# Pooled attention and a SiLU MLP in one kernel: queries transposed as pairs of 4 bytes, scores over even and odd dimensions, and two changes of order in the last tiles

## Chip, cores and metric

The kernel runs on one core of a Trainium2 chip. The metric is device time in microseconds. Before the change it is 284.45 us, the median of three runs (284.24 to 284.8). The profiled execution took 284.22 us; its profile covers a span of 282.3 us, and the TensorE clock was granted in full (1.0) throughout. All positions below are microseconds from the start of that span.

## What is computed

The reference works on 8 batches of 8 heads, 576 positions and a head dimension of 64, and then on 4608 tokens of width 512:

```python
k_p = k.reshape(B, H, Sp, 8, D).mean(axis=3)          # 576 keys pooled to 72
v_p = v.reshape(B, H, Sp, 8, D).mean(axis=3)
attn = softmax(q @ k_p.T / sqrt(D))
x = (attn @ v_p).transpose(0, 2, 1, 3).reshape(4608, 512)
h = x @ w_in                                          # 512 -> 2048
out = (h * sigmoid(h)) @ w_out                        # 2048 -> 512, float32
```

## The kernel before

**Tiles.** The MLP runs in nine tiles of 512 tokens, `t` = 0 to 8 (loop at L804). Each tile has an up phase (`up`, L470: `x @ w_in`, SiLU into `h_T`) and a down phase (`down` for tile 0, `down_quarters`, L642, for the others). The attention of batch `a = t + 1` is spread through the phases of tile `t`; batch 0 comes ahead of the loop, in a preamble (L746 to L780) in which `warm_up` matmuls fill the waits on TensorE.

**Order.** Every engine runs its instructions in the order in which the program emits them. `spread` (L416) counts the steps of a phase (a step is one or two matmuls), and a filler given as `(step, function)` is emitted right after the matmul of that step. So a number such as 71 or 103 in the loop places an instruction in the queue of its engine.

**Products with seven multiplications.** The down phase of tiles 1 to 8, and parts of the up phase, form a product of two 2x2 block matrices from seven block products instead of eight. They need sums of blocks: `hidden_sum` (L612, from `h_T` into `h_sum`), `unit_x_sum` (L452, from `xT` into `x_sum`), `weight_sum` and `unit_weight_sum`. All of them run on VectorE (DVE). In the up phase such a product is a unit, and its stages are named 2, 5, 1, 4, 3, 7, 6 for the block products, and `h` and `s` for the two SiLUs that read `c_sb`. The results of 7 and 6 pass DVE (L519, L522: `c_sb` = PSUM + `t_sb`), and `t_sb` comes from L507 and L510, so that each unit has a chain of four dependent DVE operations. `c_sb`, `t_sb` and `rr_sb` are shared by the units.

**Tiles 7 and 8** use three units, A, B and C, and four plain groups `g0` to `g3` of four 512-column matmuls (`plain`, L537). Their order is written out by hand in the strings `THREE` (L799): the first string is that of tile 7 (`t = B - 1`), the second that of tile 8. In both, the groups that a unit's SiLUs write lie in other parts of `h_T`: A and B in the upper half of each half of the hidden dimension, which the first two block products of the down phase read (L665, L666), and C and the plain groups in the lower.

**Down phase.** `down_quarters` begins with block products 2 and 5, each in two parts (upper half, then lower half), and goes on with 1, 4, 3, 7 and 6. Each needs its `h_sum`. In the last tile the block products after 5 are done for output rows 0 to 127 of each half first (`cc = (0,)`) and then for the others, so that the stores at the end are small. There, product 6 for the first rows takes steps 64 to 71, and `hidden_sum(6, 0, 4)` (L843) is placed after step 71: these matmuls are emitted ahead of the sum of that half.

**Queries.** `q_transpose` (L155) takes a tile `q_bf` whose partitions hold (head, 32 positions) and whose columns hold (i, d), and transposes 32x32 blocks of bf16 on DVE, 576 columns at a time. Four such operations serve a batch. The result `qT` is laid out `[.., i, c, p]`, where `c` is the half of the head dimension, 0 to 31 or 32 to 63, and each 32-row group of partitions is one head.

**Scores.** `scores` (L342) multiplies, for each head, the pooled keys `kz` (32 rows) with `qT` (32 rows): two matmuls, one for each `c`, add up in PSUM. Four heads lie in four row groups of the array. The keys come as `kz[.., c, :]` from `k_transpose` (L216, batches 3 to 7, out of the pooled `kp`) or `select_k` (L288, batches 0 to 2, out of `k5`).

Of the kernel before, what the change touches and what calls it, by code (L numbers as in the profile page):

```python
# [27 lines left out]
FP32 = mybir.dt.float32  # L28
FP32R = mybir.dt.float32r
BF16 = mybir.dt.bfloat16  # L30
# [6 lines left out]
def kernel(  # L37
# [11 lines left out]
    B, H, S, D = q.shape  # L49
    POOL = 8  # L50
    SP = S // POOL
# [14 lines left out]
    QP = 32  # L66
    QI = S // QP
    QF = QI // 2
    DH = D // 2
# [12 lines left out]
    singles = ctx.enter_context(tc.tile_pool(name="singles", bufs=1))  # L82
    big = ctx.enter_context(tc.tile_pool(name="big", bufs=1))
    mid = ctx.enter_context(tc.tile_pool(name="mid", bufs=2))
# [37 lines left out]


    kz = [singles.tile([128, 2, 2, SP], BF16, name=f"kz{n}") for n in range(2)]
    kp = singles.tile([128, 2, 2, 4, DH], BF16, name="kp")

    batches = {}

# [5 lines left out]
    def load_q(b, halves=False):  # L134
        st = batches.setdefault(b, {})
        q_bf = mid.tile([128, 2, QI * D], BF16, tag="q_bf", name="q_bf")
        if halves:
            pass
        elif b == B - 1:

            for s in range(4):
                for a in range(2):
                    nc.gpsimd.dma_start(
                        out=q_bf[QP * s : QP * (s + 1), a, :].rearrange(
                            "p (i d) -> p i d", d=D
                        ),
                        in_=q[b, 4 * a + s].rearrange("(i p) d -> p i d", p=QP),
                    )
        else:
            nc.gpsimd.dma_start(out=q_bf, in_=q_r[b])  # L150
        st["q_bf"] = q_bf
        st["qT"] = mid.tile([128, 2, QI, 2, QP], BF16, tag="qT", bufs=1, name="qT")


    def q_transpose(b, a, f):  # L155
        st = batches[b]
        n = QF * D
        nc.vector.transpose(  # L158
            out=st["qT"][:, a, f * QF : (f + 1) * QF].rearrange("r i c p -> r (i c p)"),
            in_=st["q_bf"][:, a, f * n : (f + 1) * n],  # L160
        )


# [28 lines left out]
    def add_rest(dst, raw):  # L192
        nc.vector.tensor_add(
            out=dst,
            in0=raw[:, :, :D].rearrange("k h (c d) -> k h c d", c=2),
            in1=raw[:, :, D : 2 * D].rearrange("k h (c d) -> k h c d", c=2),
        )

    def pool_k(b, stage):
        st = batches[b]  # L200
        raw = st["k_raw"]
        if stage == 0:
            add_halves(raw)
            return
        for i in range(2):
            add_rest(
                kp[:SP, i].rearrange("k c s d -> k s c d"), raw[:, 4 * i : 4 * (i + 1)]
            )

    def pool_v(b):  # L210
        st = batches[b]
        st["vp"] = mid.tile([SP, H, D], BF16, tag="vp", name="vp")
        add_halves(st["v_raw"])
        add_rest(st["vp"].rearrange("k h (c d) -> k h c d", c=2), st["v_raw"])

    def k_transpose(b, parts=(0, 1)):  # L216
        st = batches[b]
        kT_ps = ps_tile([128, 2, 2, SP], FP32, "at", "kT_ps")
        for a in parts:
            for c in range(2):  # L220
                nc.tensor.matmul(
                    kT_ps[:, a, c, :],
                    lhsT=kp[:, a, c].rearrange("k s d -> k (s d)"),
                    rhs=ident[:, :SP], start=True, stop=True,
                )
        a0, a1 = parts[0], parts[-1] + 1
        nc.scalar.copy(kz[b % 2][:, a0:a1], kT_ps[:, a0:a1])
# [7 lines left out]
    k5, v5 = (singles.tile([128, SLOTS + 1, D], BF16, name=f"{n}5") for n in "kv")  # L235
# [52 lines left out]
    def select_k(b, a):  # L288
        st = batches[b]
        if a == 0:  # L290
            st["kz_ps"] = ps_tile([128, 2, 2, SP], FP32, "at", "kz_ps")
        for c in range(2):
            for s in range(4):
                for i, r, sp, m in segments(4 * a + s):
                    nc.tensor.matmul(
                        st["kz_ps"][32 * s : 32 * (s + 1), a, c, sp : sp + m],
                        lhsT=k5[:, i, c * DH : (c + 1) * DH],
                        rhs=ident[:, r : r + m], start=True, stop=True,
                    )

# [31 lines left out]
    def width(segs):  # L332
        return QP * sum(i1 - i0 for _, i0, i1 in segs)
# [8 lines left out]
    def scores(b, segs):  # L342
        st = batches[b]
        w = width(segs)
        sc = [ps_tile([128, 512], FP32, "at", "sc_ps")[:SP, :w] for s in range(4)]
        for g, i0, i1, cs in seg_cols(segs):
            for c in range(2):
                for s in range(4):
                    rows = slice(32 * s, 32 * (s + 1))
                    nc.tensor.matmul(  # L350
                        sc[s][:, cs],
                        lhsT=kz[b % 2][rows, g, c, :],
                        rhs=st["qT"][rows, g, i0:i1, c, :],
                        start=(c == 0), stop=(c == 1),
                    )
        es = mid.tile([SP, 4, VW], BF16, tag="es", bufs=4, name="es")[:, :, :w]
        for s in range(4):
            nc.scalar.activation(es[:, s, :], sc[s], func=AF.Exp, scale=score_scale)  # L358
        st["es", segs] = es
# [92 lines left out]
    def unit_x_sum(t, n):  # L452
        a, b = U_X[n]
        nc.vector.tensor_tensor(
            out=x_sum[:, U_XI[n]], in0=x_quarter(t, *a), in1=x_quarter(t, *b),
            op=ALU.subtract if n in (3, 4) else ALU.add,
        )
# [154 lines left out]
    def hidden_sum(n, k0, k1):  # L612
        a, b, op = H_SUMS[n]
        ks = slice(k0, k1)
        nc.vector.tensor_tensor(  # L615
            out=h_sum[n][:, ks, :], in0=quarter(*a, ks), in1=quarter(*b, ks), op=op
        )
# [175 lines left out]
    def load_half_2(name, half):  # L793
# [1 line left out]
            load_slots(nc.gpsimd, 2, name, i0, i1, half)  # L795

    THREE = (
        "g0 A2 A5 g1 A4 B2 A3 A1 B5 A7 C2 A6 B4 B3 B1 C5 Ah B7 As C4 Bh B6 C1 C3 C7 Bs"
        " g2 C6 Ch Cs g3",  # L799
        "A2 A5 g0 A4 B2 A3 A1 B5 A7 C2 A6 B4 B3 B1 C5 Ah B7 As C4 Bh B6 C1 C3 C7 Bs g1"  # L800
        " C6 Ch Cs g2 g3",
    )
# [1 line left out]
    for t in range(NT):  # L804
        a = t + 1
        f_up, f_down = [], []
        if t == 0:
            GA = 11
            items = [(g, 0, HS) for g in range(GA)]
            items += [(g, HS, NTT - HS) for g in range(GA)]  # L810
            items += [(g, 0, NTT) for g in range(GA, KG)]
            f_up += [(1, lambda: denominators(0, part(0, 1), on_dve=True))]
            f_up += [(5, lambda: denominators(0, part(1, 1), on_dve=True))]
            f_up += [(13, lambda: numerators(0, part(0, 1)))]
            f_up += [(17, lambda: numerators(0, part(1, 1)))]
        else:
            G = lambda *gs: [(g, 0, NTT) for g in gs]
            if t == 1:
                items = (
                    G(12, 13, 14, 15) + [(0, "251")] + G(8) + [(0, "43")] + G(9)  # L820
                    + [(0, "7h6")] + G(10) + [(0, "s")] + G(11, 0, 1, 2, 3)
                )
            elif t >= B - 1:
                items = []
                for it in THREE[t - B + 1].split():
                    items += [(("BCA".index(it[0])), it[1])] if it[0] in "ABC" else G(int(it[1]))
            else:
                items = (
                    G(12, 13) + [(0, "251")] + G(14) + [(0, "43")] + G(15) + [(0, "76")]
                    + [(1, "2")] + [(0, "hs")] + [(1, "51")] + G(0) + [(1, "43")] + G(1)  # L830
                    + [(1, "7h6")] + G(2) + [(1, "s")] + G(3)
                )
            if t < B - 1:
                for n in U_X:
                    f_up.append((0, lambda n=n: unit_x_sum(t, n)))
            for n in (2, 5):
                h_at = {B - 1: 54, B: 50}.get(t, 36 if t > 1 else 45)
                f_up.append((h_at, lambda n=n: hidden_sum(n, 4, 8)))
            f_up.append((56, lambda: hidden_sum(6, 4, 8)))
            for n, k0 in ((2, 0), (5, 0), (1, 4), (1, 0)):  # L840
                f_up.append((64, lambda n=n, k0=k0: hidden_sum(n, k0, k0 + 4)))
            f_down.append((33, lambda: hidden_sum(7, 0, 8)))
            f_down.append((71, lambda: hidden_sum(6, 0, 4)))  # L843

        for n, t0, f_to, at, parts in (
            (1, 0, f_down, 48, (0, PW)), (3, 0, f_down, 52, (0, PW)),
# [61 lines left out]
                    f_down.append((nu_at[n], lambda: numerators(a - 1, visits[2])))  # L908
        if t in (B - 2, B - 1):
            for n in (4, 1, 3, 7, 6):  # L910
                f_down.append((103 if t < B - 1 else 44, lambda n=n: unit_x_sum(t + 1, n)))
        if t == B - 2:
            k_w = big.tile([128, 4, 2, 256], BF16, tag="k_raw2", name="w_sum12")
            v_w = big.tile([128, 4, 2, 256], BF16, tag="v_raw2", name="w_sum12")
# [37 lines left out]
```

The softmax here doesn't subtract the row's maximum and nothing guards it: scores larger than these inputs give would overflow.

## Time and profile before

| what | value | from |
|---|---|---|
| median time | 284.45 us | three runs |
| span of the profile | 282.3 us | page |
| preamble, up to the first matmul of tile 0 | 16.8 us | timeline of TensorE |
| tile 7, up phase to first matmul of down phase | 228.3 to 241.7 us | timeline of TensorE |
| tile 8, the same | 254.0 to 266.6 us | timeline of TensorE |
| last matmul begins, with its row of 8 | 278.2 us | timeline of TensorE |
| stores and end | 279.3 to 282.3 us | stretches of time |

The profile is a page of one execution and views of its trace. A group of instructions is told by line, engine, operation and tile, with its busy time and the mean duration of one. The chain of waits is followed back from the last instruction: at each step to what released it, or to the instruction before it on its engine. [...]what one costs in a stream is the distance between starts. A row of eight 256-column matmuls, for example, starts 0.87 us before the next row.

### The profile page before, as it was taken

What the parts mean: (1) busy time and instruction counts of PE and PEld (TensorE: products, weight loads), DVE (VectorE), ACT (ScalarE), POOL (GpSimd) and SP (SyncE); (2) the same over time, 40 slices, a digit from 0 to 9 for tenths busy, and PEclk for the clock granted to TensorE, in tenths of its full rate; (3) what the DMA queues carried; (4) which work ended last, traced back from release to release, by engine and by line L of the source; (5) the groups of instructions that cost most, each with busy time, mean ns of one, the idle gap of its engine ahead of it and who ended that gap; (6) DMA issues with size and microseconds to landing.
All of it is one profiled execution on the core that took longest, in us unless ns stands there. A gap on an engine that the chain in (4) does not pass through costs nothing.

```text
span 282.3 us, 6969 instructions
## 1 busy us (share of the span) xinstructions
PE 274.7 (97%) x2803; PEld 197.5 (70%) x2823; DVE 232.3 (82%) x418; ACT 184.5 (65%) x361; POOL 61.2 (22%) x79
## 2 busy tenths in 40 slices
PE   7899999999999999999999999999999999999995
PEld 4348544556777677767888786688667778688784
DVE  4987946899978898879887988799888978966973
ACT  1678765667577866787668856885779477326800
POOL 8745217332140214021402130441100000000001
PEclk9999999999999999999999999999999999999999
DMA  7999999896659843986397539597830041005004
GB/s 208 286 266 230 214 316 167 222 192 110 138 79 214 158 116 46 187 186 127 67 186 187 96 85 178 136 142 108 135 101 0 2 103 48 2 2 128 23 2 149
DMA packets 31312, 37.70 MB, mean 134 GB/s; under 512 B 10352, under 2 KB 22256, under 8 KB 31280
## 3 DMA queue, kind: packets, MB, share of 16 engines
q0 software_dynamic: 23920, 27.03, 53.7%
q1 hardware_dynamic: 6928, 9.58, 12.1%
q10 hardware_dynamic: 432, 0.66, 0.6%
q8 instruction: 22, 0.36, 0.5%
q14 instruction: 10, 0.08, 0.1%
HBM read 36.70 MB, written 9.44 MB: 163 GB/s over the span
## 4 chain that ended last, share of the span: by engine, by line
PE 90%; DVE 5%; DMA 2%; issue 1%; ACT 1%; DVEq 0%
PE hp_ps L547 23%; PE o_psP L655 16%; PE o_psQ L655 15%; PE u_psP L487 7%; PE u_psQ L487 7%; PE o_psR L655 5%; PE sc_ps L350 4%; PE o_ps L582 3%; PE nu_ps L394 3%; PE u_psR L487 2%; PE den_ps L368 2%; DMA raw<-in_k_dram 2%; DVE xT L403 1%; PE warm_ps L704 1%; DVE w_sum L633 1%
## 5 line engine op out<-in xcount | busy, mean ns | idle before, releaser
L547 PE MATMUL hp_ps<-xT,w_in_sb 128*128 128x512 bf16 (+3 forms) x365 | 72.3, 335 | 0.9 <-issue 0.2
L655 PEld LDWEIGHTS <-h_sum 128*128 128x128 bf16 x640 | 60.5, 98 | 12.8 <-DVE h_sum L615 1.9
L553 ACT ACTIVATE h_T<-hp_ps 128x512 bf16<-128x512 f32 (+2 forms) x87 | 46.5, 541 | 19.0 <-PE hp_ps L547 16.9
L615 DVE TENSOR_TENSOR h_sum<-h_T 128x1024 bf16<-128x1024 bf16 (+1 forms) x72 | 50.6, 745 | 5.0 <-ACT h_T L553 5.0
L547 PEld LDWEIGHTS <-w_in_sb 128*128 128x128 bf16 x380 | 36.2, 98 | 21.6 <-issue 0.6
L358 ACT ACTIVATE es<-sc_ps 72x384 bf16<-72x384 f32 (+1 forms) x100 | 39.0, 469 | 9.9 <-PE sc_ps L350 9.8
L487 PEld LDWEIGHTS <-w_sum 128*128 128x128 bf16 x340 | 33.3, 98 | 7.5
L655 PEld LDWEIGHTS <-h_T 128*128 128x128 bf16 x256 | 24.1, 98 | 4.4 <-issue 0.9
L403 DVE TENSOR_TENSOR xT<-nu_ps,rec 128x384 bf16<-128x384 f32 (+1 forms) x50 | 23.9, 532 | 0.2
L495 ACT ACTIVATE h_T<-c_sb 128x512 bf16<-128x512 f32 x34 | 20.6, 626 | 5.2 <-DVE c_sb L519 5.0
L377 ACT ACTIVATE lnd<-den_ps 128x384 f32<-128x384 f32 (+1 forms) x23 | 11.1, 483 | 19.4 <-PE den_ps L368 19.4
L158 DVE STREAM_TRANSPOSE qT<-q_bf 128x576 bf16<-128x576 bf16 x32 | 23.0, 755 | 0.6 <-DMA q_bf<-in_q_dram 0.6
L182 POOL DMA_DIRECT2D raw<-in_k_dram x5 | 7.1, 1429 | 52.1 <-DMA raw<-in_k_dram 52.1
L273 DVE TENSOR_TENSOR raw<-raw 128x384 f32<-128x384 f32 (+3 forms) x20 | 12.3, 618 | 7.2 <-DMA raw<-in_v_dram 4.1
L655 PE MATMUL o_psP<-w_out_sb,h_sum 128*128 128x256 bf16 x128 | 17.7, 273 | 0.6 <-DVE h_sum L615 0.6
L559 POOL DMA_DIRECT2D out_dram<-o_sb x2 | 1.2, 591 | 78.1 <-issue 77.3
L655 PE MATMUL o_psQ<-w_sum,h_sum 128*128 128x256 bf16 x128 | 16.7, 273 | 0.0
L504 ACT COPY r_sb<-u_psP 128x512 f32<-128x512 f32 x17 | 9.9, 584 | 10.2 <-PE u_psP L487 7.6
L655 PE MATMUL o_psQ<-w_out_sb,h_sum 128*128 128x256 bf16 x128 | 16.6, 273 | 0.0
L510 DVE TENSOR_TENSOR t_sb<-u_psR,rr_sb 128x512 f32<-128x512 f32 x17 | 11.8, 692 | 5.8 <-PE u_psR L487 4.1
L655 PE MATMUL o_psQ<-w_sum,h_T 128*128 128x256 bf16 x128 | 16.5, 273 | 0.0
L655 PE MATMUL o_psP<-w_sum,h_T 128*128 128x256 bf16 x128 | 16.5, 273 | 0.0
(83 smaller groups left out, 464.7 us busy)
## 6 DMA issues: line engine op xcount, KB each, us to landing
out_dram<-o_sb SPq DMA_DIRECT2D x128, 64.0 KB, 3.9
raw<-in_k_dram POOLq DMA_DIRECT2D x10, 576.0 KB, 9.6
raw<-in_v_dram POOLq DMA_DIRECT2D x10, 576.0 KB, 8.0
q_bf<-in_q_dram POOLq DMA_DIRECT2D x6, 576.0 KB, 12.7
w_in_sb<-in_moe_w_in_dram POOLq DMA_DIRECT2D x8, 256.0 KB, 8.6
w_out_sb<-in_moe_w_out_dram POOLq DMA_DIRECT2D x4, 512.0 KB, 13.4
raw<-in_v_dram POOLq DMA_DIRECT2D x2, 768.0 KB, 11.1
raw<-in_k_dram POOLq DMA_DIRECT2D x1, 768.0 KB, 10.3
```

The lines of the kernel that those rows point to most:

```text
L158: nc.vector.transpose(out=st["qT"][:, a, f * QF : (f + 1) * QF].rearrange("r i c p -> r (i c p)"), in_=st["q_bf"][:, a, f * n : (f + 1) * n],)
L273: nc.vector.tensor_add(out=raw[..., :w], in0=raw[..., :w], in1=raw[..., w : 2 * w])
L350: nc.tensor.matmul(sc[s][:, cs], lhsT=kz[b % 2][rows, g, c, :], rhs=st["qT"][rows, g, i0:i1, c, :], start=(c == 0), stop=(c == 1),)
L358: nc.scalar.activation(es[:, s, :], sc[s], func=AF.Exp, scale=score_scale)
L403: nc.vector.tensor_mul(out=xT[:, 2 * g0 + c : 2 * (g0 + ng - 1) + c + 1 : 2, cols], in0=nu[c][:, :w].rearrange("r (g n) -> r g n", g=ng), ...
L487: nc.tensor.matmul(ps[y, bank][:, u, :], lhsT=w[:, kk, 128 * u : 128 * (u + 1)], rhs=x[:, kk, :], start=first and u == 0 and kk == 0, stop ...
L495: nc.scalar.activation(h_T[:, g : g + 2, j * NQ : (j + 1) * NQ], src, func=AF.Silu)
L510: tt(out=t_sb, in0=ps[y, "R"], in1=rr_sb, op=ALU.subtract)
L547: nc.tensor.matmul(hp_ps[:, r0:r1], lhsT=w_in_sb[:, kk, g * 128 : (g + 1) * 128], rhs=xT[:, kk, x0 : x0 + r1 - r0], start=(kk == 0), stop= ...
L553: nc.scalar.activation(h_T[:, g, n0 : n0 + n], hp_ps[:, :n], func=AF.Silu)
L615: nc.vector.tensor_tensor(out=h_sum[n][:, ks, :], in0=quarter(*a, ks), in1=quarter(*b, ks), op=op)
L655: nc.tensor.matmul(ps[b][:, c, :], lhsT=left(n, kt, c), rhs=W_OUT[n][:, kt, :], start=b not in begun, stop=kt == k1 - 1, skip_group_check= ...
```

## The change

The queries are transposed as units of 4 bytes, that is, pairs of neighbouring bf16 values: half as many elements pass DVE. Each 32x32 block then covers 32 positions and all 64 dimensions of a head, so that `qT` is laid out `[.., i, p, 2]` and a row holds dimensions 2r and 2r + 1. The two matmuls of a score then run over the even and the odd dimensions, and read `qT` at every second element. The keys follow: `k_transpose` and `select_k` take every second column as stationary operand. `kp` has the plain layout (head, dimension), so that one DVE operation writes it instead of two.

Tile 7 gets another order of its three units, with two plain groups after `C6`, and `g0` after `A5`. The sums of x for tile 7 come at step 98 of tile 6 instead of 103, ahead of the last third of the attention. In tile 8 the sum of the lower half for product 6 comes at step 50, ahead of the matmuls that read it.

```diff
-    kp = singles.tile([128, 2, 2, 4, DH], BF16, name="kp")
+    kp = singles.tile([128, H, D], BF16, name="kp")
...
-        st["qT"] = mid.tile([128, 2, QI, 2, QP], BF16, tag="qT", bufs=1, name="qT")
+        st["qT"] = mid.tile([128, 2, QI, QP, 2], BF16, tag="qT", bufs=1, name="qT")
...
         nc.vector.transpose(
-            out=st["qT"][:, a, f * QF : (f + 1) * QF].rearrange("r i c p -> r (i c p)"),
-            in_=st["q_bf"][:, a, f * n : (f + 1) * n],
+            out=st["qT"][:, a, f * QF : (f + 1) * QF]
+            .rearrange("r i p c -> r (i p c)").bitcast(FP32),
+            in_=st["q_bf"][:, a, f * n : (f + 1) * n].bitcast(FP32),
         )
...
-        for i in range(2):
-            add_rest(
-                kp[:SP, i].rearrange("k c s d -> k s c d"), raw[:, 4 * i : 4 * (i + 1)]
-            )
+        add_rest(kp[:SP], raw)
...
-                    lhsT=kp[:, a, c].rearrange("k s d -> k (s d)"),
+                    lhsT=kp[:, 4 * a : 4 * (a + 1)].rearrange("k s d -> k (s d)")[:, c::2],
...
-                        lhsT=k5[:, i, c * DH : (c + 1) * DH],
+                        lhsT=k5[:, i, c::2],
...
-                        rhs=st["qT"][rows, g, i0:i1, c, :],
+                        rhs=st["qT"][rows, g, i0:i1, :, c],
...
     THREE = (
-        "g0 A2 A5 g1 A4 B2 A3 A1 B5 A7 C2 A6 B4 B3 B1 C5 Ah B7 As C4 Bh B6 C1 C3 C7 Bs"
-        " g2 C6 Ch Cs g3",
+        "A2 A5 g0 B2 A4 A1 A3 B5 C2 A7 B4 A6 Ah B1 B3 As C5 B7 C4 B6 Bh C1 C3 C7 Bs g1"
+        " C6 Ch Cs g2 g3",
         "A2 A5 g0 A4 B2 A3 A1 B5 A7 C2 A6 B4 B3 B1 C5 Ah B7 As C4 Bh B6 C1 C3 C7 Bs g1"
         " C6 Ch Cs g2 g3",
     )
...
-            f_down.append((71, lambda: hidden_sum(6, 0, 4)))
+            f_down.append((71 if t < B else 50, lambda: hidden_sum(6, 0, 4)))
...
-                f_down.append((103 if t < B - 1 else 44, lambda n=n: unit_x_sum(t + 1, n)))
+                f_down.append((98 if t < B - 1 else 44, lambda n=n: unit_x_sum(t + 1, n)))
```

## The prediction

> **What bounds the kernel now.** I read the busy times first, then the waits of TensorE, then the chain of waits around the few waits that are left.
>
> ```profile
> span 282.3 us, 6969 instructions
> ...
> PE 274.7 (97%) x2803; PEld 197.5 (70%) x2823; DVE 232.3 (82%) x418; ACT 184.5 (65%) x361; POOL 61.2 (22%) x79
> ```
>
> TensorE (PE) is busy 97% of the span. A busy PE may still be stretched, so I compared starts: rows of eight 256-column matmuls are 0.87 us apart in tile 2 as in tile 8 (0.109 each), a 512-column one takes 0.216, and that holds from 20.8 us on. Here are PE's waits from 20.8 to 240 us, the whole list (total, times, longest):
>
> ```profile
> PE o_ps L582 <- issue: 0.2, 1, 0.2
> PE hp_ps L547 <- issue: 0.2, 1, 0.2
> ```
>
> In 219 us PE waits for no engine. Work removed from DVE there buys nothing. What can be won lies ahead of 20.8 us and behind 240. The same view from 228 to 283 us has one wait of PE and the weight loads' waits beside it:
>
> ```profile
> PEld L655 <- DVE h_sum L615: 1.6, 4, 1.1
> ...
> PE o_psP L655 <- DVE h_sum L615: 0.6, 1, 0.6
> ```
>
> The chain of waits shows where it lies (start, us, what):
>
> ```profile
> 240.31 0.69 DVE c_sb L522
> 241.00 0.61 DVE h_sum L615
> 241.61 0.05 issue
> 241.66 1.05 PE o_psP L655 x8
> ...
> 265.07 1.73 PE hp_ps L547 x8
> 266.80 0.87 PE o_psP L655 x8
> ```
>
> At the end of tile 7's up phase the chain leaves PE for DVE and comes back at 241.66. At the same place in tile 8 it stays on PE: two plain groups (x8, 1.73 us) run while DVE makes the sum.
>
> In the preamble the chain runs through one of the changed transposes:
>
> ```profile
> 14.82 0.41 DVE vp L320
> 15.23 0.70 DVE qT L158
> 15.93 0.04 issue
> 15.97 0.44 PE sc_ps L350 x8
> 16.41 0.54 PE warm_ps L704 x2
> 16.95 0.25 PE hp_ps L547 x2
> ```
>
> **What the Trainium skill says.** "Vector Engine (DVE) Microarchitecture Reference", "The reshape front-end and per-opcode configuration": a transpose passes one element per cycle and lane, so what counts is elements, not bytes. The group below agrees for 2-byte elements; no row shows 4-byte ones. "SBUF — State Buffer", in "Door 1: The DMA port swizzle", notes lines of 16 bytes and says that one can stride for free inside them, 8 bf16 elements; here the stride is 2. No matmul of this trace reads its moving operand with a stride. "TensorE: Matmul & The Clock Gate", "Weight-path perf modes": the fast load of 128-column weights reads them "packed or strided". The trace agrees for 32 columns: L394 loads `vp` at every second column in 96 ns, L368 the contiguous `ones` in 93.
>
> **The change part by part.**
>
> Transposes:
>
> ```profile
> L158 DVE STREAM_TRANSPOSE qT<-q_bf 128x576 bf16<-128x576 bf16 x32 | 23.0, 755 | 0.6 <-DMA q_bf<-in_q_dram 0.6
> ```
>
> DVE adds in float32 take 692 ns for 512 columns (L507) and 425 for 256 (L690): 1.04 ns a column and 0.16 us fixed. 576 x 1.04 + 160 = 760, against 755, so a transpose passes one element at the same rate. With 288 elements I take 288 x 1.04 + 160 = 460 ns; if 4 bytes took two turns it stays at 755. Saved: 32 x 0.295 = 9.4 us of DVE. `kp`: five times 2 x 414 ns become one of 687 (the same form as `vp`, L193), 0.7 us. Nearly all of these 10 us are worth nothing, since PE waits for no DVE from 20.8 to 240 us.
>
> The preamble has four transposes on DVE's queue, at 7.18, 9.22, 11.73 and 15.15. The time that the first three give back is swallowed here:
>
> ```profile
> 12.69 1.15 DVE L273 TENSOR_TENSOR raw<-raw 128x512 f32<-128x512 f32 x2 [0.19 <-DMA raw<-in_v_dram]
> ```
>
> DVE already waits at 12.69 for a transfer that no edit moves (issued 4.84, 7.8 to landing); it will only wait longer. Ahead of that, PE is tied to its own warm-up matmuls and to ACT's chain. The fourth transpose, from 15.15, counts in full: it ends 0.295 earlier, PE is through with the eight `nu_ps` (from 15.29, 0.36 for such a row) at 15.65, so the scores go from 15.97 to about 15.66, the two warm-ups follow, and the first real matmul goes from 16.79 to 16.48. It needs the two L403 products too: after the transpose they start at about 15.66, when `nu_ps` is ready, at a pitch of 0.35, and end at 16.45. I take **0.29 us**. It is kept afterwards: the silus of tile 0 start behind the same scores, and the weights have landed (the third chunk of `w_in` at 20.7, needed at 22.5; the last of `w_out` at 42.6, needed at 43.4).
>
> Scores: the same 368 matmuls. A row of 16 with 192 columns takes 0.46 us; its columns, four row groups side by side, are 16 x 192 / 4 = 768 at 2.37 per ns (512 in 0.216) = 0.32. If the strided read is free, nothing changes; if it halves the rate, 0.32 a row. I take **0**, from the SBUF page. Weight loads with stride: 20 of 128 columns (98 ns) and 72 of 32 columns; upper bound the float32 load of the preamble (L708, 191 ns): 20 x 0.093 = 1.9 us. I take 0.
>
> Tile 7. In the old order, four plain matmuls run from 240.04 to 240.90, then PE stands until 241.66: 0.76 us. The next four rows of eight take 3.61 us (241.66 to 245.27), in tile 8 3.50 (266.64 to 270.14): 0.11 more, waiting for later sums. In the new order `C6` is followed by two groups, 8 x 0.216 = 1.73. From `C6`'s start to the first sum in use takes 241.66 - 239.60 = 2.06; PE has 0.44 + 1.73 = 2.17 to do. So the gap closes, with 0.11 to spare: **0.87 us** won. Does the order stall earlier? I laid the queues out by hand from the start of the phase (s = 228.28, stages of 0.437, groups 0.86): `B2`'s copy on ACT waits for `rr_sb` of A (231.2), so `A4`'s SiLU ends at 232.28, and `A7`, which needs it, is due at s + 4.36 = 232.64. `A1` needs the bank that L690 frees at 230.5, due 230.89. DVE's chain: `t_sb` of C at 237.5, its `c_sb` at 238.4, and the last `c_sb` is bound by `C6` (239.18 + 0.27 = 239.45), not by DVE. Least room 0.3 us; nothing stalls.
>
> Sums of x at step 98: they swap places with two L403 products (2 x 0.5 us); L690 behind both stays at 229.8. The delayed products free banks for `B5` (231.8) and `C2` (232.2), and would be done at 229.9. Cost 0.
>
> Tile 8's sum (0.60 pitch) now stands ahead of the copy L682: 272.80 to 273.48, so the copy ends at 273.82 instead of 273.39. Behind that copy stands product 6, which writes the same bank and was due at 273.81; 0.05 after the copy is 273.87: **0.06 us** lost, all on the path, as nothing waits between there and the stores.
>
> Sum: 0.87 + 0.29 - 0.06 = 1.10; 284.45 - 1.10 = **283.35 us**.
>
> **Rivals.**
>
> Strided reads slow the scores. For it: no row shows such a read, and PE is the bound, so every ns counts. Against: the SBUF page. At half rate: 21 rows of 192 columns x 0.32 = 6.7, and of the four 288-column rows only the last one on the path, 0.24: 283.35 + 6.9 = 290.3, slower. With a small price, 0.04 us a row, 284.2: no difference.
>
> The new order of tile 7 brings a stall of its own (a bank or ACT late by 0.3 to 0.5), while the end closes. For it: ACT is 0.7 busy there and the room 0.3. Time 283.65 to 283.9.
>
> The preamble gives nothing, because 4-byte transposes take as long, or the first matmul waits for L403: 283.6 to 283.65.
>
> **Chances.** Forecast 0.66; preamble without gain 0.08; a stall in tile 7 0.07 (a third of it within 0.2%); small price of the strides 0.07; full price 0.12. Leaving out the full price and part of the small one, the range goes to 284.2 above; below, to 282.8, for the spread of three runs (0.5 us) and a little more in the preamble. The bound of 0.2% is 0.57 us, 283.88. Faster 0.79, same 0.09, slower 0.12.
>
> **What would show it.** Transposes of 288 elements at 0.46 us; DVE busy 222; PE from the last plain matmul of tile 7 to the next without a gap, `h_sum` gone from PE's waits; first `hp_ps` at 16.5; `sc_ps` rows still 0.46 us. Rows of 0.6 us or more, or PE waiting on `h_T` or `c_sb` in tile 7's up phase, would make it wrong.

## The result, and the profile after

| | before | after |
|---|---|---|
| median time, us | 284.51 (6 runs, 284.24 to 285.54) | 283.34 (6 runs, 283.06 to 283.57) |
| span of the profile, us | 282.3 | 281.3 |
| first matmul of tile 0 | 16.79 | 16.94 |
| first matmul of tile 7's down phase | 241.66 | 240.72 |
| last row of eight begins | 278.18 | 277.20 |

The ratio is 0.9953, with a 95% interval of 0.9938 to 0.9969: 1.34 us less (0.88 to 1.76); the medians themselves are 1.17 apart. The forecast was 283.35, 1.10 us less. The total is right. Some of its parts are not: two that it had at nothing are not nothing, one was not in it, and they partly cancel.

The busy times of the page after:

```profile
span 281.3 us, 6986 instructions
...
PE 276.4 (98%) x2823; PEld 198.1 (70%) x2823; DVE 223.2 (79%) x413; ACT 184.7 (66%) x361; POOL 61.6 (22%) x79
```

DVE has 9.1 us less to do (232.3 before; the forecast had 222) and the span is 1.0 shorter. The group of the transposes, from the list of groups (busy us, mean ns):

```profile
L158 DVE STREAM_TRANSPOSE qT<-q_bf 128x288 f32<-128x288 f32 x32 | 13.4, 453 | 0.3 <-DMA q_bf<-in_q_dram 0.3
```

Half the elements take 453 ns, where the forecast had 460. From 16 us to the end the list of TensorE's waits holds a single entry (who waits for whom: total, times, longest), and its row starts in the preamble, at 15.73; in the list of all engines from 228 on, the weight loads wait for `h_sum` for 0.4 us, where it was 1.6:

```profile
PE nu_ps L391 <- DVE vp L317: 0.2, 1, 0.2
```

The chain of waits after (start, us, what), at the end of tile 7:

```profile
238.72 0.44 PE u_psQ L484 x4
239.16 1.73 PE hp_ps L544 x8
240.89 0.87 PE o_psP L652 x8
```

Tile 7 now stays on TensorE: `C6`, two plain groups, first product, as in tile 8. In tile 8's down phase, products 3, 7 and 6 of the first rows (timeline of TensorE):

```profile
270.85 1.04 PE L652 MATMUL o_psQ<-w_sum,h_T 128*128 128x256 bf16 x8
271.90 1.03 PE L652 MATMUL o_psP<-w_sum,h_sum 128*128 128x256 bf16 x8
272.83 1.03 PE L652 MATMUL o_psQ<-w_sum,h_sum 128*128 128x256 bf16 x8
```

The duration of a row, 1.04, reaches past the start of the next one, so it is the starts that count. Product 7 starts 1.05 behind product 3 and product 6 0.93 behind product 7, where an undisturbed row takes 0.87: product 7 still waits for 0.17, as before, and product 6 for 0.06, which is new. The preamble:

```profile
15.26 0.42 DVE vp L317
15.68 0.04 issue
15.73 0.43 PE nu_ps L391 x8
16.16 0.41 PE sc_ps L347 x8
```

The transpose that stood between `vp` and the scores has left the chain; `nu_ps`, which ran beside it, has taken its place. From the start of the `vp` copy to the first matmul of tile 0 it is 1.68 us (15.26 to 16.94), and 1.97 before (14.82 to 16.79). That stretch is 0.29 shorter, but it begins 0.44 later, because of a transfer: the two DVE adds that wait for it (L270 after, L273 before) come at 13.13, after a wait of 0.68, and before at 12.69, after one of 0.19. Over the profiles of this study without a doubled transpose in the preamble, the `vp` copy begins between 14.82 and 15.68 with bf16 transposes (mean of four 15.23) and between 14.83 and 15.26 with pairs (mean of seven 15.08). I read the 0.44 as the spread of the landing and not as a price of the change.

A gain that the forecast did not have lies in the down phase of tile 1. The timelines of TensorE and DVE, first before:

```profile
69.62 0.78 DVE L158 STREAM_TRANSPOSE qT<-q_bf 128x576 bf16<-128x576 bf16 x1
...
70.09 0.72 PE L350 MATMUL sc_ps<-qT,kz 32*72 32x192 bf16 x16
...
70.74 1.16 PE L655 MATMUL o_psR<-w_sum,h_sum 128*128 128x256 bf16 x9
```

and after:

```profile
69.75 0.47 DVE L158 STREAM_TRANSPOSE qT<-q_bf 128x288 f32<-128x288 f32 x1
...
70.21 0.54 PE L347 MATMUL sc_ps<-qT,kz 32*72 32x192 bf16 x16
70.67 1.16 PE L652 MATMUL o_psR<-w_sum,h_sum 128*128 128x256 bf16 x9
```

Before, the score row takes 0.65 to the start of the next row, after 0.47, as in the other tiles: its second half had waited for the transpose that ends at 70.40. Four microseconds later the same delay reaches `nu_ps` through the `vp` copy on DVE: the copy begins at 73.54 before and at 73.36 after, and the row of `nu_ps` takes 0.60 to the next start (74.10 to 74.70) before and 0.50 after (74.03 to 74.53). Together 0.29. This is the fourth transpose of tile 1, placed at step 2 of the down phase, behind the sums of tile 1 and of the weights. A row ahead of it gains 0.08 too: the first part of product 5 takes 1.05 to the next start before (66.91 to 67.96) and 0.97 after (67.11 to 68.08), because the product behind it waits for its `h_sum`. In the kernel before, DVE goes straight from the first three transposes of tile 1 (58.22 to 60.31) through `c_sb` to that sum; in the kernel after it is idle for 0.71 behind the three.

Two rows of `den_ps`, in tiles 4 and 6, get shorter as well: 0.36 and 0.37 to the next start before, 0.28 after. First tile 4's row before, then the `c_sb` of DVE ahead of it, before and after:

```profile
157.56 0.42 PE L368 MATMUL den_ps<-es,ones 72*32 72x384 bf16 x4
...
151.84 0.69 DVE L519 TENSOR_TENSOR c_sb<-u_psP,t_sb 128x512 f32<-128x512 f32 x1 [0.97 <-ACT h_T L553]
...
151.39 0.69 DVE L516 TENSOR_TENSOR c_sb<-u_psP,t_sb 128x512 f32<-128x512 f32 x1 [0.63 <-ACT h_T L492]
```

The row needs the last `es` of ACT, which ends at 157.61 before, and ACT is late because `c_sb` is: it starts 0.84 after the SiLU that ACT begins at 151.00, and after the change 0.49 after the same SiLU (150.90). These 0.35 are not work that was saved. Counted over all records of DVE in the trace, its semaphore instructions with them and from 0, the late `c_sb` of tiles 4 and 6 are numbers 319 and 447. Number 191 (`t_sb` in tile 2, at 91.09) has the same pause: it starts 0.40 after its semaphore instruction has ended, and 0.04 is usual. The three lie 128 apart. In the kernel after, these numbers fall on other operations, and none of them is held up. So the 0.17 us of the two rows come from the place where the pause falls; what makes it, the traces don't show.

One thing gets longer. A score row of tile 2, before and after:

```profile
99.57 0.53 PE L350 MATMUL sc_ps<-qT,kz 32*72 32x192 bf16 x16
...
99.42 0.54 PE L347 MATMUL sc_ps<-qT,kz 32*72 32x192 bf16 x16
```

The next row starts at 100.03 and at 99.89. Over all undisturbed rows of 16 from tile 1 on, the distance to the next start is 0.458 us before (17 rows) and 0.469 after (18 rows), and no row is more than 0.003 off. The other kernels below agree: 0.458 in each that reads `qT` without a stride, 0.469 in each that reads every second element. That is 0.0105 us a row, 0.22 us for the 21 rows of 192 columns. The strided reads are not quite free.

### The profile page after: what moved, and what is told of

The parts are those of the page before. It is cut to its first block, busy times and chain, and to the rows that moved or that the text cites. A ratio compares the mean times of both kernels' runs of the same rounds, so it can differ in the third digit from the quotient of the medians.

```text
span 281.3 us, 6986 instructions
## 1 busy us (share of the span) xinstructions
PE 276.4 (98%) x2823; PEld 198.1 (70%) x2823; DVE 223.2 (79%) x413; ACT 184.7 (66%) x361; POOL 61.6 (22%) x79
## 4 chain that ended last, share of the span: by engine, by line
PE 92%; DVE 3%; DMA 2%; ACT 1%; issue 1%; DVEq 0%
PE hp_ps L544 24%; PE o_psP L652 15%; PE o_psQ L652 15%; PE u_psP L484 8%; PE u_psQ L484 8%; PE o_psR L652 5%; PE sc_ps L347 4%; PE o_ps L579 3%; PE nu_ps L391 3%; PE u_psR L484 3%; PE den_ps L365 2%; DMA raw<-in_k_dram 2%; PE warm_ps L701 1%; DVE xT L400 1%; DVE w_sum L630 1%; DVE raw L270 1%
## 5 line engine op out<-in xcount | busy, mean ns | idle before, releaser
L544 PE MATMUL hp_ps<-xT,w_in_sb 128*128 128x512 bf16 (+3 forms) x380 | 74.5, 337 | 0.1
L270 DVE TENSOR_TENSOR raw<-raw 128x384 f32<-128x384 f32 (+3 forms) x20 | 12.4, 619 | 9.4 <-DMA raw<-in_v_dram 6.1
L516 DVE TENSOR_TENSOR c_sb<-u_psP,t_sb 128x512 f32<-128x512 f32 x17 | 11.7, 690 | 8.4 <-ACT kz L224 4.2
L652 PE MATMUL o_psP<-w_sum,h_T 128*128 128x256 bf16 x128 | 16.5, 273 | 0.0
L652 PE MATMUL o_psQ<-w_sum,h_T 128*128 128x256 bf16 x128 | 16.5, 273 | 0.0
L504 DVE TENSOR_TENSOR rr_sb<-u_psQ,r_sb 128x512 f32<-128x512 f32 x17 | 11.7, 691 | 5.6 <-ACT r_sb L501 5.0
```

The source lines that it names most:

```text
L270: nc.vector.tensor_add(out=raw[..., :w], in0=raw[..., :w], in1=raw[..., w : 2 * w])
L504: tt(out=rr_sb, in0=ps[y, "Q"], in1=r_sb, op=ALU.add)
L516: tt(out=c_sb[0], in0=ps[y, "P"], in1=t_sb, op=ALU.add)
L544: nc.tensor.matmul(hp_ps[:, r0:r1], lhsT=w_in_sb[:, kk, g * 128 : (g + 1) * 128], rhs=xT[:, kk, x0 : x0 + r1 - r0], start=(kk == 0), stop= ...
L652: nc.tensor.matmul(ps[b][:, c, :], lhsT=left(n, kt, c), rhs=W_OUT[n][:, kt, :], start=b not in begun, stop=kt == k1 - 1, skip_group_check= ...
```

## Experiments

Each ran beside the kernel before; ratios are against it. A gain in us is what the ratio lacks to 1, times that median, 284.6 to 284.7.

**e1: only the order.** The kernel before with the new string of tile 7 and the sums of x at step 98.

```diff
 (kernel before)
-        "g0 A2 A5 g1 A4 B2 A3 A1 B5 A7 C2 A6 ... Bs g2 C6 Ch Cs g3",
+        "A2 A5 g0 B2 A4 A1 A3 B5 C2 A7 B4 A6 ... Bs g1 C6 Ch Cs g2 g3",
-                f_down.append((103 if t < B - 1 else 44, ...
+                f_down.append((98 if t < B - 1 else 44, ...
```

> The kernel before with the new order of tile 7 alone (string of the units and the sums of x at step 98); transposes, keys and scores as before. Theory (the parts add up): the 0.76 us gap at the end of tile 7's up phase and the 0.11 us in the four rows behind it go, nothing else moves: 0.87 us less than before, ratio 0.997; the preamble and tile 1 as before. Rival (the gap closes only because DVE has less to do with pair transposes): the gap stays at 0.5 us or more, ratio 0.999.

Measured: 283.89 (12 runs), ratio 0.9975 (0.9966 to 0.9984): 0.71 us, with 0.87 inside the interval. In the trace the two plain groups begin at 240.04 and the first product at 241.77, 1.73 later, without a wait. Tile 1 gains nothing here.

**e2: only the pairs.** The kernel after, with the old string, 103 and 71.

```diff
 (kernel after)
-        "A2 A5 g0 B2 A4 A1 A3 B5 C2 A7 B4 A6 ... Bs g1 C6 Ch Cs g2 g3",
+        "g0 A2 A5 g1 A4 B2 A3 A1 B5 A7 C2 A6 ... Bs g2 C6 Ch Cs g3",
-                f_down.append((98 if t < B - 1 else 44, ...
+                f_down.append((103 if t < B - 1 else 44, ...
-            f_down.append((71 if t < B else 50, lambda: hidden_sum(6, 0, 4)))
+            f_down.append((71, lambda: hidden_sum(6, 0, 4)))
```

> The changed kernel with the old order of tile 7, the sums of x at step 103 and the last sum at step 71: transposes as pairs, strided scores and keys alone. Theory: 0.30 us less in the preamble (scores of its fourth part at 0.25 us less after the vp copy) and 0.31 us less in the down phase of tile 1 (the second scores and the numerators no longer wait on DVE), gap of 0.76 us in tile 7 as before: 0.6 us less than before, ratio 0.998. Rival (only the preamble counts; what moved in tile 1 was chance): 0.3 us less, the stall in the scores of tile 1 still there. Second rival (strided reads cost 10 ns a row of scores): 0.4 us less, rows of scores 0.47 instead of 0.46.

Measured: 284.26 (21 runs), ratio 0.9987 (0.998 to 0.9993): 0.37 us (0.20 to 0.57). The trace has the 0.3 of the preamble and the 0.3 of tile 1, and tile 7's gap of 0.76 is back. That makes 0.6, just outside the interval. The second rival is right about the rows: the next row starts 0.469 after them and not 0.458, 0.22 us in all. The theory left this out, as it did the 0.25 that tile 1's earlier row and tiles 4 and 6 give here too. What is lost lies in tile 8:

```profile
270.55 0.69 DVE L667 TENSOR_TENSOR rr_sb<-o_psQ,r_sb 128x512 f32<-128x512 f32 x1 [0.67 <-PE o_psQ L652]
```

It begins 0.61 after the start of the next row on TensorE, in all the other profiles of this study 0.26, and product 7 (273.09) then waits 0.36 for the copy L674 behind it. This `rr_sb` is number 575 of DVE's records: the pause of tiles 4 and 6, which here falls where TensorE feels it. From the `vp` copy to the last row of eight the trace of e2 takes 0.27 less than that of the kernel before, which is 0.29 + 0.38 + 0.17 - 0.22 - 0.35. By the times, e1 and e2 add up to 1.08 against 1.34 for the whole, within the intervals; that pause, which the kernel after doesn't have there, is of the size of the rest.

**e3: tile 8's string in tile 7.** Is it only the two groups at the end that count, or also the order of the units?

```diff
 (kernel before)
-        "g0 A2 A5 g1 A4 B2 A3 A1 B5 A7 C2 A6 ... Bs g2 C6 Ch Cs g3",
+        "A2 A5 g0 A4 B2 A3 A1 B5 A7 C2 A6 ... Bs g1 C6 Ch Cs g2 g3",
```

> The kernel before with the string of tile 8 in tile 7 too, sums of x left at step 103. Theory (what counts is that two plain groups stand behind C6; the order of the units ahead of it and the step of the sums of x do not matter): same gain as the new order, 0.87 us, ratio 0.997. Rival (the new order of the units or the earlier sums of x are needed, because A4 would wait for the sums of x): a stall of 0.2 us or more near the start of tile 7, gain 0.6 us or less.

Measured: 283.96 (9 runs), ratio 0.9979 (0.9969 to 0.9988), 0.60 us. The gap at the end is closed (groups at 239.72, product at 241.44), but a new one opens at the beginning. The timeline:

```profile
230.73 0.60 PE L487 MATMUL u_psP<-xT,w_sum 128*128 128x256 bf16 x4
231.43 0.60 PE L487 MATMUL u_psQ<-x_sum,w_in_sb 128*128 128x256 bf16 x4
```

`B2` starts at 230.73 and its turn of 0.44 ends at 231.17; `A3` (the second line) follows at 231.43. It writes the bank that `rr_sb` (L507) reads from 230.70 to 231.38. So 0.26 are lost, and 0.87 - 0.26 = 0.61 agrees with the median; the interval (0.34 to 0.88) alone would not rule out 0.87.

**e9: the same, and the sums of x at step 98.**

```diff
 (kernel before, with tile 8's string in tile 7)
-                f_down.append((103 if t < B - 1 else 44, ...
+                f_down.append((98 if t < B - 1 else 44, ...
```

> The kernel before with tile 8's string in tile 7, as in the earlier run of that string, but with the sums of x at step 98. The stall of 0.26 us in that run stood ahead of A3: A3 writes the bank that rr_sb reads (L507), and rr_sb stands on DVE's queue behind the sums of x and the last add of tile 6 (L690). Theory: the sums of x only swap places with two products of L403, so L690 and rr_sb stay where they were, and the stall of 0.26 stays: ratio 0.998 again (-0.60 us), A3 at the same distance behind A1's matmuls. Then the order of B2, A4, A1, A3 in the new string is what removes it. Rival: the earlier sums of x are what removes it; ratio 0.997 (-0.87).

Measured: 283.93 (7 runs), ratio 0.997 (0.9959 to 0.9982), 0.85 us. The times can't tell the theory from the rival (both are in the interval), but the trace can:

```profile
230.98 0.60 PE L487 MATMUL u_psP<-xT,w_sum 128*128 128x256 bf16 x4
231.55 0.60 PE L487 MATMUL u_psQ<-x_sum,w_in_sb 128*128 128x256 bf16 x4
```

`A3` stands 0.57 behind `B2`, in e3 0.70, unhindered 0.44. Half of the stall is gone: neither the theory nor the rival has it all. Measured from the last attention row of tile 6 (`nu_ps`, 227.01 in e3 and 227.25 here), the last add of tile 6 (L690) begins after 2.97 instead of 3.09. So the sums of x don't only swap places, as I had written: with them between the two pairs of L403, DVE does the same work in 0.12 less. In e3 the four L403 stand in one piece of 1.99 from start to next start; here they are two pieces of 0.94 and 0.93. The likely reason is that the third had waited for the `nu_ps` before it; the list of waits doesn't show it. The other 0.13 are left to the order `B2 A4 A1 A3`, in which one more stage stands ahead of `A3`. In the kernel after that order alone would do: `rr_sb` ends there at 230.79 and `A3` starts at 231.15, so 0.12 more would fit.

**e4: one group behind `C6` instead of two.**

```diff
 (kernel after)
-        "A2 A5 g0 ... Bs g1 C6 Ch Cs g2 g3",
+        "A2 A5 g0 ... Bs g1 g2 C6 Ch Cs g3",
```

> The changed kernel with one plain group moved back ahead of C6 in tile 7 (g1 g2 C6 Ch Cs g3), the new order of the units kept. Theory: PE stands 0.76 us at the end of tile 7's up phase again, and 0.1 in the rows behind: 0.87 us more than the changed kernel, 0.5 us less than before, ratio 0.998. Rival (the new order of the units shortens the chain on DVE, and the group counts little): the gap is 0.4 us or less.

Measured: 284.19 (21 runs), ratio 0.9983 (0.9976 to 0.9989). The chain of waits of e4 leaves TensorE at the place where it left it before:

```profile
239.71 0.70 DVE c_sb L519
240.41 0.02 issue
240.44 0.64 ACT h_T L492
```

TensorE has `C6` ahead of them (239.17, 0.45) and comes back at 241.08. As before, it stands 0.76 between the last plain matmul and the first product (240.30 to 241.06 by the starts). The path is bound by `C6` itself, then the add, the SiLU and the sum, not by a DVE queue that is late: `c_sb` starts 0.09 after `C6` has had its turn. So two groups are what it takes, as the forecast's comparison of 2.17 with 2.06 had it.

**e5: transposes of batches 3 to 7 issued twice.** DVE gets 20 of them more.

```diff
 (kernel after)
-                f_to.append((q_at[n], lambda n=n: q_transpose(a, n % 2, n // 2)))
+                for _ in range(2 if a > 2 else 1):
+                    f_to.append((q_at[n], lambda n=n: q_transpose(a, n % 2, n // 2)))
```

> The changed kernel with every transpose of batches 3 to 7 issued twice: 20 more of 0.47 us, 8 to 9 us more on DVE in tiles 2 to 6. Theory (PE waits for no DVE there, so what the transposes saved in these tiles was worth nothing): same time as the changed kernel within 0.1 us, ratio to before 0.996. Rival (DVE at 79 to 82% busy has no room, the savings in these tiles were part of the gain): 0.3 us or more lost, stalls of PE on h_sum or qT in tiles 2 to 6.

Measured: 283.35 (6 runs), ratio 0.9953 (0.994 to 0.9967), the same as after. The transposes (x52, mean 463 ns) keep DVE busy for 23.0 us, as much as in the kernel before, and nothing is lost: from tile 2 on the length of these transposes is worth nothing. It is close, though: in tile 2 the doubled pair ends at 99.03 and the scores that read it start at 99.10.

**e8: two transposes twice, the fourth of the preamble and the fourth of tile 1.** If the gain lies in two of the 32, putting back just these should take it away.

```diff
 (kernel after)
     q_transpose(0, 1, 1)
+    q_transpose(0, 1, 1)
...
+                for _ in range(2 if (t, n) == (1, 3) else 1):
```

> The changed kernel with just two transposes issued twice, the fourth of the preamble and the fourth of tile 1. Theory (these two of the 32 carry the whole gain of the transposes): 0.3 us lost in the preamble and 0.2 to 0.3 in tile 1, 0.5 to 0.6 us more than the changed kernel, ratio to before 0.998. Rival (the gain is spread, or what shifted in tile 1 was chance): 0.1 us or less lost.

Measured: 284.34 (22 runs), ratio 0.9987 (0.998 to 0.9993). It loses 0.97 of the 1.34, more than expected, because a second transpose into the same part of `qT` costs 0.51 and not the 0.30 by which the bf16 form was longer. From the `vp` copy to the first matmul it is 2.19 (15.54 to 17.73), 0.51 more than after; tile 1 loses 0.51 as well.

**e10: only that of tile 1 twice.** e8 without the second line in the preamble.

```diff
 (kernel after)
-                f_to.append((q_at[n], lambda n=n: q_transpose(a, n % 2, n // 2)))
+                for _ in range(2 if (t, n) == (1, 3) else 1):
+                    f_to.append((q_at[n], lambda n=n: q_transpose(a, n % 2, n // 2)))
```

> The kernel after, with the fourth transpose of tile 1 alone issued twice (a doubled transpose took 0.51 us more where two were doubled). Theory: this transpose stands ahead of the scores of tile 1's second third and of the copy of vp, and its length is worth the 0.31 us that tile 1 gained; doubled, it costs 0.3 to 0.5 there and nothing elsewhere: ratio 0.9965 to 0.9972 against the kernel before, first matmul of tile 0 as in the kernel after, a gap in the score row near 70 us. Rival: the tile 1 gain came from work ahead of it on DVE or from chance; then doubling costs under 0.15 and the ratio stays at 0.9953 to 0.9958.

Measured: 283.75 (5 runs), ratio 0.9965 (0.9952 to 0.9977), 0.34 us lost against after by the times. By the trace, tile 1 loses 0.51 (0.41 in the score row and 0.10 in the row of `nu_ps`), a little more than expected. The first matmul of tile 0 is where it should be (1.68 behind the start of the `vp` copy), and the timeline shows the gap at the score row:

```profile
70.24 0.36 PE L347 MATMUL sc_ps<-qT,kz 32*72 32x192 bf16 x8
70.82 0.37 PE L347 MATMUL sc_ps<-qT,kz 32*72 32x192 bf16 x8 [0.21 <-DVE qT L158]
```

The two transposes start at 69.78 and take 0.98; the second half of the scores waits for them. So it was in the kernel before, with 0.30 in place of 0.51. The 0.29 at these two rows of tile 1 come from the length of this transpose.

**e6: how far may the score's stride go?** The scores of batches 4, 5, 6 and 7 read `qT` at every 4th, 6th, 8th and 9th element (so at other data); batches 0 to 3 stay at 2.

```diff
 (kernel after)
+    STEP = {4: 4, 5: 6, 6: 8, 7: 9}
...
-                        rhs=st["qT"][rows, g, i0:i1, :, c],
+                        rhs=st["qT"].rearrange("r g i p c -> r (g i p c)")[
+                            rows, c : c + STEP[b] * (QP * (i1 - i0) - 1) + 1 : STEP[b]
+                        ] if b in STEP else st["qT"][rows, g, i0:i1, :, c],
```

> The changed kernel, whose scores read qT at other strides in four batches, so that the output is not the reference's: batch 4 at every 4th element (8 bytes), batch 5 at every 6th (12 bytes), batch 6 at every 8th (16 bytes), batch 7 at every 9th (18 bytes); batches 1 to 3 at every second as before. Theory (free inside a line of 16 bytes): rows of 16 scores 0.46 to 0.47 us in batches 1 to 5, and longer from batch 6 on, 0.6 us or more at a whole line per element. Rival (a stride of 2 already costs, and more with each step): 0.46 contiguous, 0.47 at 2, rising steadily with the stride. Second rival (no stride costs anything here): 0.47 in all.

Measured: 292.48 in one run. One row each of stride 2, 4 and 8, from the timeline (start, duration of the row of 16):

```profile
105.84 0.54 PE L349 MATMUL sc_ps<-qT,kz 32*72 32x192 bf16 x16
...
124.43 0.86 PE L349 MATMUL sc_ps<-qT,kz 32*72 32x192 bf16 x16
...
185.71 1.53 PE L349 MATMUL sc_ps<-qT,kz 32*72 32x192 bf16 x16
```

Rows of stride 6 take 1.20, of stride 9 1.57.

Stride 2 takes 0.54, where contiguous reads took 0.53. Each further step of 2 elements (4 bytes) adds 0.32 to 0.34, which is one more streaming of the row's 768 columns (0.32 in the prediction's working); from 8 to 9 it adds 0.04. Three rows a batch, 3 x (0.32 + 0.66 + 0.99 + 1.03) = 9.0 us, account for the 9.1 by which the run is longer than the kernel after.

**e7: the waits that are left in tile 8.** The sums of the last tile for products 7 and 6 are split into halves of 128 columns, so that each half of the output rows waits for its own only.

```diff
 (kernel after)
-    def hidden_sum(n, k0, k1):
+    def hidden_sum(n, k0, k1, cs=slice(0, NQ)):
...
-            f_down.append((33, lambda: hidden_sum(7, 0, 8)))
-            f_down.append((71 if t < B else 50, lambda: hidden_sum(6, 0, 4)))
+            if t < B:
+                f_down.append((33, lambda: hidden_sum(7, 0, 8)))
+                f_down.append((71, lambda: hidden_sum(6, 0, 4)))
+            else:
+                for c in range(2):
+                    cs = slice(128 * c, 128 * (c + 1))
+                    f_down.append((33 + 24 * c, lambda cs=cs: hidden_sum(7, 0, 8, cs)))
+                    f_down.append((50 + 15 * c, lambda cs=cs: hidden_sum(6, 0, 4, cs)))
```

> The changed kernel with the sums 7 and 6 of the last tile done in two halves of 128 columns, the half that the first rows read first: in the last tile product 7 waits 0.17 us for the copy behind the whole sum 7, and product 6 0.06 us for the copy behind the sum 6. Theory: both waits go, 0.2 us less than the changed kernel (span 281.1 where the transfers of the preamble come alike). Rival (two more operations on DVE bring the same wait elsewhere in the last tile): no gain.

Measured: 283.09 (5 runs), ratio 0.9941 (0.9928 to 0.9954), faster than the kernel before by 1.68 us. Products 7 and 6 of the first rows in the timeline:

```profile
271.41 1.04 PE L653 MATMUL o_psP<-w_sum,h_sum 128*128 128x256 bf16 x8
272.28 1.04 PE L653 MATMUL o_psQ<-w_sum,h_sum 128*128 128x256 bf16 x8
```

Product 3 ahead of them starts at 270.54, so all three starts are 0.87 apart: both waits are gone, and from the first product of tile 8 to the last row it takes 11.37 instead of 11.60 us. That it beats the kernel after by these 0.23 is shown by the traces; the intervals of the times overlap.

## Why the prediction was right, and where it was not

| step of the prediction | forecast, us | the traces |
|---|---|---|
| the preamble's fourth transpose | -0.29 | -0.29 (1.97 to 1.68) |
| DVE's other savings, 20.8 to 240 us | 0 | -0.38 in tile 1 (0.30 for the fourth transpose, 0.08 ahead of it) |
| a pause on DVE that falls elsewhere, tiles 4 and 6 | not in it | -0.17 |
| strided reads | 0 | +0.22 |
| strided weights | 0 | 0 |
| order of tile 7 | -0.87 | -0.76 and -0.10 |
| sums of x at step 98 | 0 | 0 in this order (-0.13 with tile 8's, e3 and e9) |
| tile 8's sum ahead of the copy | +0.06 | +0.06 |
| sum | -1.10 | -1.42; times: -1.34 (-1.76 to -0.88) |

Tile 1's 0.30 is its 0.29 with the 0.01 by which its score row got dearer. From the `vp` copy to the last row of eight the traces have 263.36 us before and 261.94 after, the same 1.42. That the median lies within 0.01 us of the forecast is luck: the parts that the forecast lacked come to -0.33 in the traces, and the kernel before has a median of 284.51 over six runs, not 284.45.

**Tile 7** came as worked out. From the last `nu_ps` row of tile 6 to the first product it was 14.93 (226.73 to 241.66) and is 14.17 (226.55 to 240.72); the four rows after it took 3.61 and take 3.51. e4 shows that the forecast's limit, `C6` and what hangs on it, is the right one. The rival of a new stall is refuted for the new string, and true for its neighbour: with tile 8's string the stall that I had looked for in ACT's queue came from DVE's (`rr_sb` behind the last add of tile 6). This wait, of `A3` for `rr_sb`, was not on my list. In the kernel after its room is 0.36 (`rr_sb` ends at 230.79, `A3` starts at 231.15).

**The preamble** too. That its first real matmul is at 16.94 and not at 16.5 has to do with where the stretch begins. The prediction would have done better to name the distance from the `vp` copy than a position.

**The step that failed** is "In 219 us PE waits for no engine. Work removed from DVE there buys nothing". The list of waits was empty, but three rows of tile 1 were longer by 0.19, 0.10 and 0.08 than they are after, and two of tiles 4 and 6 by 0.08 and 0.10; I had compared starts in tiles 2 and 8 only. The page's row for `sc_ps` is a group of all such rows, in which one of 0.72 among 0.53 doesn't show. What sets tile 1 apart is the length of DVE's queue at the start of its down phase: the sums of the weights stand in it too, ahead of the transpose. For the transposes of tiles 2 to 6 the conclusion holds, as e5 shows with 20 more. "Nearly all of these 10 us are worth nothing" stands in this sense: two transposes of 32, 0.6 us of saving, gave 0.59 us, and e8 takes it away again. That the 0.08 of tile 1 belong to its first three transposes is read from the timeline; no run doubles them alone.

**The strided reads** were taken at 0, and that failed too: they cost 0.0105 us a row of 0.458, 0.22 us in all, the rival of a small price at a quarter of the 0.04 us that I had put down for it. The gains that I had missed hid it. The reason for the 0 doesn't hold either. In the Trainium skill, "SBUF — State Buffer", "Door 1: The DMA port swizzle", one may stride for free up to 8 bf16 elements inside a line of 16 bytes. e6 differs: 4 elements already take 0.32 us a row more than 2, 8 take 0.99. For a matmul's moving operand of this form a step of 4 bytes is nearly free, and the change uses all of it: there was no margin. The strided weights (98 ns for `kp` in both kernels) cost nothing, as the skill's "TensorE: Matmul & The Clock Gate", "Weight-path perf modes", let expect.

## What to carry to other kernels

An empty list of waits is not the same as an engine without waits: compare the distances of starts, row by row, in every tile that differs from the others (the first ones above all), before work on another engine is called worthless. The same distances, averaged over many rows, show a price of 0.01 us that a duration of two decimals hides. Of an operation that gets shorter 32 times, look for the few whose reader is next in line; doubling exactly these shows whether the gain is theirs. And where a layout puts a stride into a matmul's operand, measure the next larger stride too: it tells how much room is left.

## What the runs showed of the hardware

- A row of 16 matmuls that read their moving operand at every 2nd bf16 takes 0.469 us to the next start, contiguous 0.458. At every 4th, 6th and 8th element its duration is 0.86, 1.20 and 1.53 us instead of 0.54, at every 9th 1.57.
- A DVE transpose of 4-byte elements passes them at the rate of 2-byte ones: 453 ns for 288, against 755 for 576.
- A transpose followed by another DVE operation takes 0.40 from start to start (69.75 to 70.15 in tile 1), one followed by another into a different part of the same tile 0.36 to 0.40 (58.41 on). A second one into the same part adds 0.51 (69.78 to 70.69 for two in e10): it starts only after the first has ended.
- On DVE, operations that had to wait for a semaphore start about 0.35 us late where they stand at certain numbers of its records, 128 apart: 191, 319 and 447 in the kernel before, 575 in e2 and e5, 191 and 319 in e10. Where DVE runs on without a wait, as at these numbers in the kernel after, nothing shows. The pause can reach TensorE: 0.35 us in e2. Its cause is open.
